# A fused forward-and-backward kernel: two loads re-ordered on one queue, and the last product cut in two

## The chip, the core and the metric

The kernel runs on one core of a Trainium2 chip. Such a core has a matrix engine (TensorE, "PE" in the profile, with its weight loads as "PEld"), a vector engine (VectorE, "DVE"), a scalar engine (ScalarE, "ACT"), GpSimd ("POOL"), and SyncE ("SP"), which here does nothing but issue transfers. Sixteen DMA engines move the data. Operands lie in an on-chip memory of 128 partitions; a matmul writes to PSUM, from which ScalarE or VectorE copies the result. The metric is the device time of one launch in microseconds (us), the lower the better.

## The reference, cut to what matters

Two branches read a layer-normed `x` (2048 rows of 512): a gated convolution along the sequence (branch A) and a bilinear feed-forward layer of width 1376 (branch B). The kernel computes the output and the gradients of nine inputs.

```python
xn = layernorm(A_q)
# branch A
k_shift = sum_t k_pad[:, t:t+S, :] * shift_k[:, ks-1-t]      # ks = 4 taps
kv = k_shift * v
y  = causal_convolution(kv, ssm_k) + kv * ssm_D              # by FFT in the reference
A  = xn * y
# branch B
h  = (xn @ w_gate) * (xn @ w_up)
B  = h @ w_down
out = A_q + A + B
outputs = out, and the gradients to A_q, A_k, A_v, shift_k, ssm_k, ssm_D, w_gate, w_up, w_down
```

In the code below, `out_9` is the gradient to `w_down` (1376 x 512), `out_7` and `out_8` are those to `w_gate` and `w_up` (512 x 1376), `out_5` is that to `ssm_k`, `out_4` that to `shift_k`, `out_0` the output, and `out_1`, `out_2`, `out_3` the gradients to `A_q`, `A_k` and `A_v`.

## The kernel before, in words

The 2048 rows lie as 128 partitions x 16 rows (`R = 16`). In the first 300 us, eight chunks of 256 rows go through the feed-forward layer (`ffn1`, `yb`), and beside them a transform of the convolution's operands runs through DRAM buffers. Two of those buffers matter here: `HDD` holds, for eleven blocks of 128 hidden columns (the last has 96), the hidden values `h` and two gradients; `GD` holds the spectral products.

From 300 us on, `dw()` (L1044) takes the eleven blocks `fb` of `HDD` in turn. For each, `down_grad(fb)` (L1022) makes `pd`, 16 matmuls of 512 columns (`out_9`), and then `pu`, 64 matmuls, gives the gradients of the other two weights (`og`, L1069). Blocks 0 to 5 come by a plain load `load_hb` (L790, into tiles `hb`, two buffers) and are turned on TensorE by `hid_t` (L846, matmuls of L859): parts 0 and 1 of block `fb + 1` behind block `fb`'s `pd`, part 2 in the middle of block `fb + 1`'s own `pd`. Blocks 6 to 10 are turned by the transfer itself (`load_t`, L804, tile `natT`).

Between these, generators on a hand-written cadence (`sides`, L1197) put other work: `inv_y` (L944) turns the spectral products back, by loads `load_g1` (L783, tile `g1`; the profile calls it `g`) and matmuls `pq` (L932): for every four rows `r4` once into `yC`, once into `dd`, which VectorE multiplies by `vb` into `dks` (L962) and by `kb` (L963). `dsk_gram` (L1079) multiplies `dks` by the shifted k (`khC`, matmuls `pk`, L1085), for `out_4`. `ew` (L1180) runs `final(b)` (L1127: `o`, `e`, by VectorE, with the load `bb`) and `bwd(b)` (L1104: `tk`, `dk`), and stores `o`, `e`, `dk` one turn later (`put_late`, L1177).

From 300 us on, transfers are asked for on SyncE's queue, but for two that are on ScalarE's: the last `BX` store, and half of the last `out_9` store (L1039). A scheduler in the framework orders the instructions of each engine by its own estimate of their times; `tc.issue_after(x)` keeps a transfer behind transfer `x`; `tc.high_priority` pulls instructions ahead. Transfers take eight completion semaphores in turn: the ninth waits until the first has landed.

Three places are touched by the change:

- `open_c` (L862) asks, at about 300 us, for `hb` of block 0, for two `g1` tiles, and then for `hb` of block 1.
- `load_kh` (L1156) asks for the shifted k: one load of 2 MB and two small ones. `inv_y` calls it at the end of its turn `r4 = 8` (`R - 8`), and the loads are kept behind the last `g1` load (`LG["g"]`).
- `down_grad(10)`, the last block (96 columns), is the last work of TensorE. Its `pd` is copied out in two halves of 256 columns, one by ScalarE and one by VectorE (L1035 to L1039); the two `og` stores of this block are asked for by SyncE (L1073) just before.

Of the kernel before, what the change touches and what calls it, by code (L numbers as in the profile page):

```python
# [8 lines left out]
BF = mybir.dt.bfloat16  # L9
# [9 lines left out]
D = 512  # L19
F = 1376  # L20
R = 16
P = 128
NC4 = 4
FBLK = [(i * 128, min(128, F - i * 128)) for i in range((F + 127) // 128)]
NFB = len(FBLK)
# [165 lines left out]
def kernel(  # L191
# [24 lines left out]
    nc = tc.nc  # L216
# [14 lines left out]
    def cs(c):  # L231
        return slice(c * 128, (c + 1) * 128)

    def act(o, i):
        nc.scalar.copy(o, i)  # L235
# [10 lines left out]
    HDD = dram.tile([P, NFB, NCH - 1, 3, 256], BF, name="HDD")  # L246
# [5 lines left out]
    def P2(name, shape, dt=F32):  # L252
        return ps2.tile(shape, dt, name=name, tag="p2")

    def P1(name, shape, dt=F32):
        return ps1.tile(shape, dt, name=name, tag="p1")
# [526 lines left out]
    def load_g1(sg, r0):  # L783
        t = CP["b"].tile([P, 2, 4, D], BF, name="g1")
        LG["g"] = nc.sync.dma_start(t[:], GD[sg, :, :, r0:r0 + 4, :])
        return t

    LG = {}

    def load_hb(fb):  # L790
        f0, fw = FBLK[fb]
        t = CP["b"].tile([P, NCH - 1, 3, 256], BF, name="hb")
        nc.sync.dma_start(t[:fw], HDD[:fw, fb])
        hbs[fb] = t

    hbs = {}
# [37 lines left out]
    def nat_h(fb, r):  # L834
        f0, fw = FBLK[fb]
        if fb not in TURNED:
            return nats[fb, 0][:, r, :fw]
        return nats[fb, 0][r // 2][:, 0, r % 2, :] if r < R - 2 else nats[fb, 1][:, 0, r % 2, :fw]

    def nat_d(fb, r):  # L840
        f0, fw = FBLK[fb]
        if fb not in TURNED:
            return nats[fb, 1][:, :, r, :fw]
        return nats[fb, 0][r // 2][:, 1:3, r % 2, :] if r < R - 2 else nats[fb, 1][:, 1:3, r % 2, :fw]

    def hid_t(fb, t):  # L846
        if fb in TURNED:
            return
        f0, fw = FBLK[fb]
        hb = hbs.pop(fb) if t == 2 else hbs[fb]  # L850
        if t == 0:
            nats[fb, 0] = CP["n"].tile([P, R, P], BF, name="nath")
        elif t == 1:
            nats[fb, 1] = CP["n"].tile([P, 2, R, P], BF, name="natd", bufs=2)
        dst = nats[fb, 0] if t == 0 else nats[fb, 1][:, t - 1]
        pt = P2("pt", [P, R, P], BF)
        for r in range(R):
            hs = hb[:fw, r // 2, t] if r < R - 2 else hds[1][:fw, fb, t]
            nc.tensor.transpose(pt[:, r, :fw], hs[:, (r % 2) * 128:(r % 2) * 128 + 128], ident[:fw, :fw])  # L859
        act(dst[:, :, :fw], pt[:, :, :fw])  # L860

    def open_c():  # L862
        for _ in side:
            pass
        gpool["es"].close()
        CP["n"] = ctx.enter_context(tc.tile_pool(name="c1n", bufs=1, reuse_waits="tile"))
        CP["b"] = ctx.enter_context(tc.tile_pool(name="c1b", bufs=2, reuse_waits="tile"))
        load_hb(0)
        pend.extend((load_g1(0, 0), load_g1(1, 0)))
        load_hb(1)  # L870

    def main():
        for ch in range(NCH):
# [22 lines left out]
    for tag in mainit:  # L896
        if tag == "wa":
# [3 lines left out]
            goC = c1.tile([P, R, D], BF, name="goC")  # L901
# [15 lines left out]
    c2b = ctx.enter_context(tc.tile_pool(name="c2b", bufs=2, side="right", reuse_waits="tile"))  # L917
# [10 lines left out]
    def st1p(g, i0, dst):  # L928
        pq = P2("pq", [P, 2, D])
        for i in range(2):  # L930
            for c in range(2):
                nc.tensor.matmul(pq[:, i, :], lhsT=TB.IW[:, c, :], rhs=g[:, c, i0 + i, :], start=(c == 0), stop=(c == 1))  # L932
        act(dst, pq[:])

    def load_vk(r0):
        vb = c2b.tile([P, 2, D], BF, name="vb")
        nc.sync.dma_start(vb[:], v_n[:, r0:r0 + 2, :])
        kb = c2b.tile([P, 2, D], BF, name="kb")
        DKS["kb", r0] = nc.sync.dma_start(kb[:], KS[:, r0:r0 + 2, :])
        return vb, kb  # L940
# [3 lines left out]
    def inv_y():  # L944
        gq = pend
        todo = [(sg, r0) for r0 in range(0, R, 4) for sg in (0, 1)][2:]
        for r4 in range(0, R, 4):
            gy = gq.pop(0)
            vk = [load_vk(r4), load_vk(r4 + 2)]
            for i in range(0, 4, 2):  # L950
                st1p(gy, i, yC[:, r4 + i:r4 + i + 2, :])
            if todo:
                gq.append(load_g1(*todo.pop(0)))
            yield
            gd = gq.pop(0)
            for i in range(0, 4, 2):
                r0 = r4 + i
                vb, kb = vk.pop(0)
                dd = c2b.tile([P, 2, D], BF, name="dd")
                st1p(gd, i, dd[:])  # L960
                with tc.high_priority(offset=SOON):
                    nc.vector.tensor_tensor(dks[:, r0:r0 + 2, :], dd[:], vb[:], op=ALU.mult)  # L962
                    nc.vector.tensor_tensor(kb[:], dd[:], kb[:], op=ALU.mult)  # L963
                DKS[r0] = nc.sync.dma_start(o3_n[:, r0:r0 + 2, :], kb[:])
                if r0 == 2:
                    nc.gpsimd.memset(dks[96:128, R:R + 3, :], 0.0)
                    nc.sync.dma_start(dks[0:112, R:R + 3, :], dks[1:113, 0:3, :])
                    nc.sync.dma_start(dks[112:127, R:R + 3, :], dks[113:128, 0:3, :])
            if todo:
                gq.append(load_g1(*todo.pop(0)))  # L970
            if r4 == R - 8:
                load_kh()
            yield

    def load_gk(rq):
# [45 lines left out]

    def down_grad(fb):  # L1022
        f0, fw = FBLK[fb]
        pd = P1("pd", [P, D])
        for r in range(R):
            nc.tensor.matmul(pd[:fw, :], lhsT=nat_h(fb, r), rhs=goC[:, r, :], start=(r == 0), stop=(r == R - 1))  # L1026
            if r == R // 2 - 1 and fb:
                hid_t(fb, 2)
                if fb + 2 < NFB:
                    load_h(fb + 2)  # L1030
        od = c2b.tile([P, D], BF, name="od")
        if fb + 1 < NFB:
            act(od[:fw], pd[:fw])
            nc.sync.dma_start(out_9[f0:f0 + fw, :], od[:fw])
        else:  # L1035
            for h, cp, q in ((0, act, nc.scalar), (1, dve, nc.sync)):
                hc = slice(256 * h, 256 * h + 256)
                cp(od[:fw, hc], pd[:fw, hc])
                q.dma_start(out_9[f0:f0 + fw, hc], od[:fw, hc])  # L1039

    def load_h(fb):
        (load_t if fb in TURNED else load_hb)(fb)

    def dw():  # L1044
        og = None
        load_hb(2)
        for fb, (f0, fw) in enumerate(FBLK):
            last = fb + 1 == NFB
            if not last:
                down_grad(fb)  # L1050
                yield
                hid_t(fb + 1, 0)
                hid_t(fb + 1, 1)
                yield
                yield
            pu = P2("pu", [P, NC4, 2, P])
            if fb % 2 == 0:
                og = c2b.tile([P, 2, NC4, P], BF, name="og1", tag="dd") if last else c2.tile([P, 2, NC4, 2 * P], BF, name="og")
            q0 = (fb % 2) * P
            for c in range(NC4):  # L1060
                for r in range(R):
                    nc.tensor.matmul(pu[:, c, :, :fw], lhsT=xnC[:, r, cs(c)], rhs=nat_d(fb, r),  # L1062
                                     start=(r == 0), stop=(r == R - 1))
                if c == 1:
                    yield
                    if fb + 1 in TURNED:
                        last_t(fb + 1)
                    yield
            act(og[:, :, :, q0:q0 + fw].rearrange("p t c f -> p c t f"), pu[:, :, :, :fw])  # L1069
            if fb % 2 == 1 or last:  # L1070
                a = f0 - q0
                for t, o in enumerate((out_7, out_8)):
                    LG["og"] = nc.sync.dma_start(o[:, a:f0 + fw].rearrange("(c p) f -> p c f", p=128), og[:, t, :, :q0 + fw])  # L1073
            yield
            if last:
                down_grad(fb)
                yield
# [78 lines left out]
    def load_kh():  # L1156
        khC = c2.tile([P, R + 3, D], BF, name="khC", tag="o5k")
        nc.gpsimd.memset(khC[0:1, 0:3, :], 0.0)
        with tc.issue_after(LG["g"].ins):
            nc.sync.dma_start(khC[:, 3:3 + R, :], k_n)  # L1160
            nc.sync.dma_start(khC[1:113, 0:3, :], k_n[0:112, R - 3:R, :])
            nc.sync.dma_start(khC[113:128, 0:3, :], k_n[112:127, R - 3:R, :])
        KH.append(khC)
# [72 lines left out]
```

## Time and profile before

| what | value |
|---|---|
| device time, median of 3 runs | 479.41 us (476.85 to 480.81) |
| the profiled execution: its own time | 479.29 us |
| its span (first to last instruction) | 477.5 us |
| granted TensorE clock over the span | 0.998 |
| TensorE busy, 300 to 470 us | 168.9 of 170 us |
| moved by DMA, mean | 139.85 MB, 293 GB/s |

A row of the page's part 2 has 40 slices of about 12 us; each digit is a busy share in tenths. A line of the timeline has the start, the time taken (us), the engine (`SPq` and `ACTq` are the queues that issue transfers: that time is the issuing alone), the line of the kernel, the operation, what it writes and reads, its count, and in brackets how long the engine had been idle and what ended that. "To landing" is the time from a transfer's issue until it has arrived.

### The profile page before, as it was taken

What the parts mean: (1) busy time and instruction counts of PE and PEld (TensorE: products, weight loads), DVE (VectorE), ACT (ScalarE), POOL (GpSimd) and SP (SyncE); (2) the same over time, 40 slices, a digit from 0 to 9 for tenths busy, and PEclk for the clock granted to TensorE, in tenths of its full rate; (3) what the DMA queues carried; (4) which work ended last, traced back from release to release, by engine and by line L of the source; (5) the groups of instructions that cost most, each with busy time, mean ns of one, the idle gap of its engine ahead of it and who ended that gap; (6) DMA issues with size and microseconds to landing.
All of it is one profiled execution on the core that took longest, in us unless ns stands there. A gap on an engine that the chain in (4) does not pass through costs nothing.

```text
span 477.5 us, 10282 instructions
## 1 busy us (share of the span) xinstructions
PE 461.4 (97%) x4206; PEld 308.9 (65%) x4247; DVE 339.8 (71%) x610; ACT 304.1 (64%) x356; POOL 13.9 (3%) x30
## 2 busy tenths in 40 slices
PE   7998999999999999999999999999999999999995
PEld 6876765547637538447547753467776787777884
DVE  7889988979447566787857878112147898799892
ACT  4957777749567678879779975275775654333330
POOL 8000000000000000000000000110000000000000
PEclk9999999999999999999999999999999999999999
DMA  9999999998998968968968459998999999999948
GB/s 267 377 373 372 290 286 321 328 313 295 324 292 284 263 189 273 284 193 259 300 218 261 155 198 371 327 366 301 337 371 381 366 304 311 319 284 299 229 166 269
DMA packets 116916, 139.85 MB, mean 293 GB/s; under 512 B 44775, under 2 KB 90248, under 8 KB 115462
## 3 DMA queue, kind: packets, MB, share of 16 engines
q1 hardware_dynamic: 115286, 137.85, 90.8%
q10 hardware_dynamic: 1584, 1.36, 1.0%
q8 instruction: 33, 0.54, 0.5%
q14 instruction: 13, 0.11, 0.1%
HBM read 65.70 MB, written 63.41 MB: 270 GB/s over the span
## 4 chain that ended last, share of the span: by engine, by line
PE 77%; DMA 12%; DVE 6%; issue 1%; SPq 1%; ACT 1%; DVEq 0%; ACTq 0%
PE pu L1062 14%; PE px L555 13%; PE pgu L512 13%; PE pd L1026 8%; PE py L548 6%; PE pdh L518 6%; PE pt L859 3%; PE pq L932 3%; PE ps L584 3%; PE pg L613 3%; DMA ssk<-in_A_ssm_k_dram 3%; PE pf L370 2%; DMA hb<-HDD 2%; DMA x_b<-in_A_q_dram 2%; DMA XN<-x_b 1%
## 5 line engine op out<-in xcount | busy, mean ns | idle before, releaser
L555 PE MATMUL px<-WT,hd 128*128 128x512 bf16 (+1 forms) x340 | 78.6, 379 | 1.6 <-issue 1.4
L1062 PEld LDWEIGHTS <-xnC 128*128 128x128 bf16 x704 | 67.1, 98 | 8.2 <-issue 0.4
L555 PEld LDWEIGHTS <-hd 128*128 128x128 bf16 (+1 forms) x352 | 32.8, 98 | 44.4 <-issue 7.7
L235 ACT CAST gu<-pgu 128x1024 bf16<-128x1024 f32 (+1 forms) x48 | 45.4, 946 | 16.5 <-PE pgu L512 16.2
L235 ACT CAST GO<-pg 128x1024 bf16<-128x1024 f32 x48 | 46.3, 1016 | 13.7 <-issue 7.2
L235 ACT CAST SP<-ps 128x1024 bf16<-128x1024 f32 x47 | 45.6, 1027 | 13.7 <-PE ps L584 11.8
L512 PE MATMUL pgu<-xt,Wu 128*128 128x256 bf16 (+1 forms) x352 | 53.2, 273 | 1.2 <-DVE kn L238 0.6
L600 DVE TENSOR_TENSOR T<-SP 128x2048 bf16<-128x2048 bf16 x24 | 29.4, 1223 | 34.8 <-ACT SP L235 34.7
L512 PE MATMUL pgu<-xt,Wg 128*128 128x256 bf16 (+1 forms) x352 | 52.8, 273 | 0.0
L518 PE MATMUL pdh<-gt,WdT 128*128 128x256 bf16 (+1 forms) x352 | 46.9, 273 | 0.1
L235 ACT CAST fst<-pf 128x1024 bf16<-128x1024 f32 x44 | 42.8, 1032 | 5.8 <-issue 2.3
L1062 PE MATMUL pu<-natd,xnC 128*128 128x256 bf16 x384 | 43.9, 273 | 0.0
L512 PEld LDWEIGHTS <-Wu 128*128 128x128 bf16 (+1 forms) x352 | 33.0, 100 | 15.5 <-issue 10.6
L548 PE MATMUL py<-Wd,hd 128*128 128x512 bf16 (+1 forms) x167 | 40.2, 380 | 0.8 <-issue 0.5
L518 PEld LDWEIGHTS <-WdT 128*128 128x128 bf16 (+1 forms) x352 | 34.9, 100 | 4.8 <-issue 0.2
L512 PEld LDWEIGHTS <-Wg 128*128 128x128 bf16 (+1 forms) x352 | 34.8, 100 | 3.8 <-DMA Wg<-in_B_w_gate_dram 0.2
L1062 PE MATMUL pu<-natT,xnC 128*128 128x256 bf16 (+1 forms) x280 | 32.3, 267 | 0.0
L533 DVE TENSOR_TENSOR hd<-gu,dh 128x1024 bf16<-128x1024 bf16 (+1 forms) x48 | 30.8, 642 | 0.8
L532 DVE TENSOR_TENSOR hd<-gu 128x512 bf16<-128x512 bf16 (+1 forms) x48 | 19.1, 398 | 16.1 <-ACT gu L235 16.1
L548 PEld LDWEIGHTS <-hd 128*128 128x128 bf16 (+1 forms) x176 | 16.5, 98 | 20.8 <-issue 3.1
L235 ACT CAST og<-pu 128x1024 bf16<-128x1024 f32 (+1 forms) x11 | 10.9, 993 | 29.7 <-PE pu L1062 22.1
L600 DVE TENSOR_TENSOR U<-SP 128x2048 bf16<-128x2048 bf16 x24 | 29.2, 1219 | 0.0
(175 smaller groups left out, 680.9 us busy)
## 6 DMA issues: line engine op xcount, KB each, us to landing
HDD<-hd SPq DMA_DIRECT2D x35, 384.0 KB, 4.4
FD<-fst SPq DMA_DIRECT2D x24, 512.0 KB, 5.2
X<-FD SPq DMA_DIRECT2D x24, 512.0 KB, 5.2
GD<-GO SPq DMA_DIRECT2D x24, 512.0 KB, 3.7
g<-GD SPq DMA_DIRECT2D x11, 1024.0 KB, 8.0
hb<-HDD SPq DMA_DIRECT2D x6, 1344.0 KB, 11.2
bb<-BX SPq DMA_DIRECT2D x8, 512.0 KB, 5.6
BX<-bx SPq DMA_DIRECT2D x7, 512.0 KB, 3.9
```

The lines of the kernel that those rows point to most:

```text
L235: nc.scalar.copy(o, i)
L512: nc.tensor.matmul(pgu[:w, i, t, :], lhsT=W[:, c, f0:f0 + w], rhs=xt[:, :, c, :], start=(c == 0), stop=(c == NC4 - 1))
L518: nc.tensor.matmul(pdh[:w, i, :], lhsT=WdT[:, c, f0:f0 + w], rhs=gt[:, :, c, :], start=(c == 0), stop=(c == NC4 - 1))
L532: nc.vector.tensor_tensor(hd[:fw, fb0:fb0 + n, 0, :], gu[:fw, :n, 0, :], gu[:fw, :n, 1, :], op=ALU.mult)
L533: nc.vector.tensor_tensor(hd[:fw, fb0:fb0 + n, 1:3, :], gu[:fw, :n], dh[:fw, :n].unsqueeze(2).to_broadcast((fw, n, 2, 256)), op=ALU.mult)
L548: nc.tensor.matmul(py[:], lhsT=hd[:fw, fb, 0, ss], rhs=Wd[:fw, fb, :], start=(fb == 0), stop=(fb == NFB - 1))
L555: nc.tensor.matmul(px[:], lhsT=hd[:fw, fb, t, ss], rhs=W[:fw, fb, :], start=(t == 1 and fb == 0), stop=(t == 2 and fb == NFB - 1))
L584: nc.tensor.matmul(ps[32 * q:32 * q + 32, a, :], lhsT=TB.EF[64 * a:64 * a + 64, 4 * g + q, ri].rearrange("p k j -> p (k j)"), rhs=X[64 * a ...
L600: tt(W[:].rearrange("p c a d -> p c (a d)"), A[:, i:i + 1].rearrange("p c a d -> p c (a d)").to_broadcast((P, 2, 2 * D)), B[:].rearrange(" ...
L613: nc.tensor.matmul(pg[q // 2][64 * a:64 * a + 64, q % 2, :], lhsT=TB.EI[32 * q:32 * q + 32, 2 * g + a, yi].rearrange("p k c -> p (k c)"), ...
L1026: nc.tensor.matmul(pd[:fw, :], lhsT=nat_h(fb, r), rhs=goC[:, r, :], start=(r == 0), stop=(r == R - 1))
L1062: nc.tensor.matmul(pu[:, c, :, :fw], lhsT=xnC[:, r, cs(c)], rhs=nat_d(fb, r), start=(r == 0), stop=(r == R - 1))
```

## The change

```diff
 def load_hb(fb):
-        nc.sync.dma_start(t[:fw], HDD[:fw, fb])
+        LG[fb] = nc.sync.dma_start(t[:fw], HDD[:fw, fb])
...
 def open_c():
         load_hb(0)
+        load_hb(1)
         pend.extend((load_g1(0, 0), load_g1(1, 0)))
-        load_hb(1)
...
 def inv_y():
         for r4 in range(0, R, 4):
             gy = gq.pop(0)
+            if r4 == R - 4:
+                load_kh()
             vk = [load_vk(r4), load_vk(r4 + 2)]
...
-            if r4 == R - 8:
-                load_kh()
             yield
...
 def down_grad(fb):
+        if fb + 1 == NFB:
+            for h, q in ((0, nc.sync), (1, nc.scalar)):
+                hc = slice(256 * h, 256 * h + 256)
+                pd = P1("pd", [P, 256])
+                for r in range(R):
+                    nc.tensor.matmul(pd[:fw, :], lhsT=nat_h(fb, r), rhs=goC[:, r, hc], start=(r == 0), stop=(r == R - 1))
+                od = c2b.tile([P, D], BF, name="od")
+                act(od[:fw, :256], pd[:fw])
+                q.dma_start(out_9[f0:f0 + fw, hc], od[:fw, :256])
+            return
...
-        if fb + 1 < NFB:
-            act(od[:fw], pd[:fw])
-            nc.sync.dma_start(out_9[f0:f0 + fw, :], od[:fw])
-        else:
-            for h, cp, q in ((0, act, nc.scalar), (1, dve, nc.sync)):
-                hc = slice(256 * h, 256 * h + 256)
-                cp(od[:fw, hc], pd[:fw, hc])
-                q.dma_start(out_9[f0:f0 + fw, hc], od[:fw, hc])
+        act(od[:fw], pd[:fw])
+        nc.sync.dma_start(out_9[f0:f0 + fw, :], od[:fw])
...
 def dw():
-                    LG["og"] = nc.sync.dma_start(o[:, a:f0 + fw]...)
+                    LG["og"] = (nc.scalar if last else nc.sync).dma_start(o[:, a:f0 + fw]...)
...
 def load_kh():
-        with tc.issue_after(LG["g"].ins):
+        with tc.issue_after(LG[5].ins):
```

- The load of block 1's `hb` goes ahead of the two `g1` loads.
- The three loads of the shifted k are asked for one turn of `inv_y` later (`r4 = 12`), and are kept behind block 5's `hb` load. In the changed program SyncE's order there is: last `g1` load, `o` and `e` stores, `bb` load, block 5's `hb`, `out_9`'s store, then the three `khC` loads, then `vb` and `kb`.
- The last block's `pd` is two products of 16 matmuls of 256 columns in place of one of 16 of 512. Both halves are copied by ScalarE; SyncE stores the first and ScalarE the second. The last block's two `og` stores move from SyncE's queue to ScalarE's, ahead of these copies.
- As the scheduler works from its own estimates, VectorE's order changes too, in one place: the two first instructions of `final(2)` (`o`, `e`) and its addition of `bb` move up among the end of `final(1)` and `bwd(0)`, and the `dks` and `kb` products of `r4 = 12`, which stood before `bwd(1)`, come right after it. TensorE's order differs in the last product alone, ScalarE's in the last copies and stores.

More of the change, by code (lines that the diff above doesn't have):

```diff
@@ L1072, in dw @@
                 for t, o in enumerate((out_7, out_8)):
-                    LG["og"] = nc.sync.dma_start(o[:, a:f0 + fw].rearrange("(c p) f -> p c f", p=128), og[:, t, :, :q0 + fw])
+                    LG["og"] = (nc.scalar if last else nc.sync).dma_start(o[:, a:f0 + fw].rearrange("(c p) f -> p c f", p=128), og[:, t, :, :q0 + fw])
             yield
```

## The prediction, made before the changed kernel was run

> **What bounds the kernel now.** First the page: busy time by engine, and the DMA row.
>
> ```profile
> PE 461.4 (97%) x4206; PEld 308.9 (65%) x4247; DVE 339.8 (71%) x610; ACT 304.1 (64%) x356; POOL 13.9 (3%) x30
> DMA  9999999998998968968968459998999999999948
> ```
>
> TensorE is busy for 97% and the DMA engines nearly as long. All edits lie after 300 us, so I asked for TensorE's waits from 320 us to the end. The answer is one line:
>
> ```profile
> PE pd L1026 <- issue: 0.2, 1, 0.2
> ```
>
> So no load makes TensorE wait there; before that, at 308.36 us, 0.21 us was spent on block 0's `hb`, which the change does not touch. What remains of the two moved loads is margins. The timeline gives when TensorE first reads each of them:
>
> ```profile
> 318.40 1.89 PE L932 MATMUL pq<-g,IW 128*128 128x512 bf16 x8
> 320.12 0.94 PE L859 MATMUL pt<-ident,hb 128*128 128x128 bf16 x14
> ...
> 384.69 0.94 PE L859 MATMUL pt<-ident,hb 128*128 128x128 bf16 x14
> ...
> 390.06 1.94 PE L1085 MATMUL pk<-khC,dks 128*64 128x256 bf16 x32
> ```
>
> These are the first `g`, block 1's `hb`, block 5's `hb`, and the first use of `khC`.
>
> **Block 1's `hb` ahead of `g`: 0.** By issue time plus time to landing, the queue delivers in order: `hb` 0 at 308.3 (300.15 + 8.2), `g` at 310.8 and 313.4, `hb` 1 at 316.6 (302.39 + 14.2). The same bytes in the new order: `hb` 1 lands 3.2 us after `hb` 0, at 311.5, the first `g` 2.5 later, at 314.0, the second at 316.6. They are needed at 320.1, 318.4 and 325.4 us: margins of 8.6, 4.4 and 8.8 us where they were 3.5, 7.6 and 12. Nothing waited and nothing will. The next load in that queue, block 2's `hb`, needs a buffer that TensorE frees at 315, and stays there.
>
> **`khC` behind block 5's `hb`: 0 on TensorE.** SyncE's queue there:
>
> ```profile
> 363.66 0.53 SPq L785 DMA_DIRECT2D g<-GD  x1
> 364.24 0.60 SPq L1160 DMA_DIRECT2D khC<-in_A_k_dram  x1
> ...
> 366.08 0.38 SPq L1177 DMA_DIRECT2D out_dram<-o  x1
> ...
> 367.77 0.49 SPq L793 DMA_DIRECT2D hb<-HDD  x1
> ...
> 375.91 0.33 SPq L937 DMA_DIRECT2D vb<-in_A_v_dram  x1
> ```
>
> The transfers are full there (DMA share 0.92 to 1.06 from 365 to 385), so landings follow the order of bytes. Before: `g` 369.6, `khC` 375.9 and 376.6, `hb` 5 at 383.4 (367.77 + 15.6), which leaves 1.3 us before 384.69; `vb`, `kb`, `vb` at 384.4, 385.0 and 385.7. After: `o`, `e` and `bb` go ahead of 2.4 MB of `khC`, 0.65 us for each 256 KB (`vb` to `kb`) or 1.1 (`khC` to `o`, which VectorE waited for until 377.7), so `o` lands at 370.3 to 370.7, `e` by 371.8, `bb` by 374. `hb` 5 can be asked for when TensorE frees its buffer (366.6) and lands near 376.5, 8 us early. `khC` is asked for behind `out_9`'s store, which stood at 369.7, and lands at about 383.7, 6.4 us before 390.06. `vb` and `kb` end where they did, as the sum of bytes is the same. The 5.9 us that SyncE waited before `vb` for `khC`'s landing (it takes the completion semaphore of the transfer eight before it) goes too, but the data could not have come sooner. In a slower execution 1.3 us of margin on `hb` 5 could be too little and 6.4 on `khC` would not be; here I count nothing.
>
> **VectorE's new order: 0, with a thin margin.** Before:
>
> ```profile
> 371.62 0.69 DVE L1151 TENSOR_TENSOR e<-e,goC 128x1024 bf16<-128x1024 bf16 x1
> ...
> 377.72 0.69 DVE L1135 TENSOR_TENSOR o<-xnC,yC 128x1024 bf16<-128x1024 bf16 x1 [0.84 <-DMA out_dram<-o]
> 378.95 0.69 DVE L1139 TENSOR_TENSOR e<-goC,yC 128x1024 bf16<-128x1024 bf16 x1 [0.53 <-DMA out_dram<-e]
> 380.22 0.69 DVE L1136 TENSOR_TENSOR o<-o,bb 128x1024 bf16<-128x1024 bf16 x1 [0.58 <-DMA bb<-BX]
> ...
> 387.65 0.69 DVE L962 TENSOR_TENSOR dks<-dd,vb 128x1024 bf16<-128x1024 bf16 x1
> ```
>
> The three waits (1.95 us) were for transfers queued behind `khC`, and go. But the `dks` products of `r4 = 12` now come after `bwd(1)`. From 371.62 I add the distances between starts: `o`, `e`, `e` and `o`+`bb` 0.61 each; two `bwd` of 4.6; the rest of `final(2)` 5.6. That puts the last `dks` product at 390.0, done at 390.7, where it was done at 388.3. The gram takes 32 matmuls in 1.87 us, row by row, and reads rows 14 and 15 in its last eighth, from 391.7. The margin falls from 3.4 to 1.0 us. GpSimd's order is unchanged. On SyncE's queue the second `kb` store (390.81) waits for its product until 391.4 now, and `dk`, `bb` and `og` behind it may come 0.5 us late; VectorE alone waits for these. Then `o` of `final(3)` waits for a store asked for behind the turning load at 389.2, and the next `bb` (396.97) comes when it did or 0.5 later, so VectorE's gain of 1.95 us is gone by 397.
>
> **The tail: -0.3.**
>
> ```profile
> 471.87 2.07 SPq L1073 DMA_DIRECT2D out_dram<-og  x2
> 472.38 0.37 ACT L235 CAST od<-pd 96x256 bf16<-96x256 f32 x1 [2.60 <-PE pd L1026]
> 472.78 0.36 ACTq L1039 DMA_DIRECT2D out_dram<-od  x1
> 472.78 0.42 DVE L238 CAST od<-pd 96x256 bf16<-96x256 f32 x1 [4.42 <-ACT od L235]
> 474.04 0.64 SPq L1039 DMA_DIRECT2D out_dram<-od  x1
> ```
>
> TensorE ends at 472.3. VectorE's copy waits for ScalarE's, then SyncE is still issuing `og`, and the last store leaves 1.26 us after ScalarE's. In the semaphores' records `og` lands at 476.0 and 476.4, ScalarE's half at 475.8, SyncE's at 476.6; the closing waits take the other 0.9 us to 477.5. After: ScalarE copies `og` until 469.8 and issues its two stores by 470.6 (0.4 each, as on ScalarE's queue at 472.78) or 471.8 (1.0 each, as on SyncE's at 471.87). The first half of `pd` ends at 470.6, its copy at 472.2 at the latest, and SyncE stores it once `dk` is issued (471.8). The second half ends at 472.4: 32 matmuls of 256 columns cost what 16 of 512 do, since `pu`'s 32 took 3.49 us and `pd`'s 16 took 3.47. Its copy (0.37) and issue follow at 472.8, as before. So the issuing is 1.26 us shorter. Does the end follow? The DMA engines' rows say hardly:
>
> ```profile
> 472.00:473.00 1.00, 0.34 (x2) 0.00 (x0) 0.22 (x1) 0.37 (x1) 0.00 (x0) 1.00 1.01 397
> ...
> 475.00:476.00 1.00, 0.00 (x0) 0.00 (x0) 0.00 (x0) 0.00 (x0) 0.00 (x0) 0.58 1.01 178
> ```
>
> The share is 0.97 to 1.09 in every microsecond from 470 to 476: the engines work off one backlog (`o5t`, `dk`, `og`) without a gap, and the bytes stay. By that row the gain is 0. The other bound is a last half that lands 3.0 us after its issue, as ScalarE's did (472.78 to 475.8), which gives 475.9 instead of 476.6: -0.75. I take -0.3, nearer the full engines.
>
> A rule of the Trainium skill says otherwise of the halves: "TensorE: Matmul & The Clock Gate", section "The mechanism", has weight loads run beside matmuls only when their row groups differ. By it sixteen more weight loads would be paid in full; `pu`'s 3.49 us with its 32 loads of 98 ns beside it disagree.
>
> The sum, on the profiled execution: 479.29 + 0 + 0 + 0 - 0.3 = **479.0 us**, 0.4 under the median of 479.41.
>
> **Rivals.**
>
> *The tail gives all of its issue time:* the small `og` packets go between `o5t`'s large ones and cost nothing. For it: DMA share above 1 at 470 to 472, so packets overlap somewhat. Against: in 475 to 476 two queues were active and the rate was 178 GB/s. It is -0.75, 478.5 us. Chance 0.15.
>
> *Hidden stalls of other executions go:* the three runs spread from 476.85 to 480.81, and block 5's `hb` had 1.3 us to spare. Were half of the upper spread such stalls, the median falls to some 478. Chance 0.12. Nothing in this trace shows one.
>
> *Slower, VectorE's order:* `o` now stands ahead of `e`+`goC`, `bwd(0)` and, further on, the `dks` products, so a late store of `final(0)` holds them all, and TensorE waits at the first gram. It decides from a landing at 372.6 (371.62 + 1.0), 8.4 us after the issue at 364.2; beyond, each microsecond costs one. At the landing before (377.7) it would be 5.1 us: 484.4 us. Against: 256 KB right behind a `g` that lands at 369.6. Chance 0.06 for over 0.5 us, half of that for over 4.
>
> *Slower, paid weight loads:* 16 x 0.098 = 1.6 us on TensorE, so the last store is issued at 474.4, lands at 477.4 and ends 0.8 later than now: 480.1 us. Chance 0.04.
>
> *Nothing changes that can be measured, since no wait was there to remove:* that is my forecast, with 0.63.
>
> **How the numbers follow.** The three runs spread over 0.8%, so 1%, 4.8 us, is about what a measurement can tell from no change. All cases but the far end of the order's stay within it: slower 0.04 (0.03 from that end, 0.01 for two small ones together), faster 0.05 (the outer part of the hidden stalls' 0.12, where they are longer than the three runs show), same 0.91. The range takes the tail's bounds (-0.75 to +0.8) and the spread of the runs about their median (-2.6 to +1.4): 476.0 to 481.4.
>
> **What would show it.** Right: TensorE without a wait from 320 us on; `hb` 5 landing near 376 and `khC` near 384; VectorE without the three waits at 377 to 381; the last landing between 475.9 and 476.6. Wrong: a wait of `pk` on `dks` or `khC` near 390, a gap before `pq` at 318, `pd`'s 32 matmuls over 3.6 us, or DMA share under 0.9 before the end.

## The result, and the profile after

| kernel | device time, median | lowest to highest | runs |
|---|---|---|---|
| before | 479.47 us | 476.85 to 482.54 | 22 |
| after | 481.70 us | 479.03 to 484.63 | 22 |

The ratio after to before is 1.0042, 95% interval 1.0024 to 1.0059: the change makes the kernel slower by 2.0 us. The forecast was 479.0 and its range ended at 481.4; the median lies 0.3 above that, and the movement has the other sign. It is within the 1% that was called "same".

The profiled execution of the changed kernel took 479.56 us (span 477.7), the second fastest of the 22. That it is as short as the profile of before is luck of its first part: TensorE comes to the matmuls `pq` of `r4 = 12` 1.57 us earlier in it. First the line of before, then that of the changed kernel:

```profile
375.12 1.89 PE L932 MATMUL pq<-g,IW 128*128 128x512 bf16 x7
...
373.55 1.89 PE L932 MATMUL pq<-g,IW 128*128 128x512 bf16 x8
```

From TensorE's `pq` at 318.40 (316.82 in the changed kernel) to this one the two take the same time, 56.7 us. From this `pq` to the end of the span are 102.4 us before and 104.2 after. So two profiles are better compared by times counted from this `pq`; where the text does so, it says it. The page's busy times and the DMA row of the changed kernel:

```profile
PE 465.4 (97%) x4263; PEld 310.9 (65%) x4263; DVE 339.0 (71%) x609; ACT 304.3 (64%) x357; POOL 13.9 (3%) x30
...
DMA  8999999988998968967977459998999999999959
```

As before: TensorE is at 97%. Of TensorE's waits from 320 us on there is again one line:

```profile
PE pu L1066 <- ACT natd L235: 0.2, 1, 0.2
```

No load makes TensorE wait, as forecast. The timeline of VectorE, of the changed kernel, answers to the lines of before with the three waits and the last `dks` product:

```profile
369.72 0.69 DVE L1139 TENSOR_TENSOR o<-xnC,yC 128x1024 bf16<-128x1024 bf16 x1
...
373.27 0.69 DVE L1140 TENSOR_TENSOR o<-o,bb 128x1024 bf16<-128x1024 bf16 x1
...
388.10 0.68 DVE L964 TENSOR_TENSOR dks<-dd,vb 128x1024 bf16<-128x1024 bf16 x1
...
392.40 0.69 DVE L1139 TENSOR_TENSOR o<-xnC,yC 128x1024 bf16<-128x1024 bf16 x1 [3.00 <-DMA out_dram<-o]
...
397.17 0.69 DVE L1140 TENSOR_TENSOR o<-o,bb 128x1024 bf16<-128x1024 bf16 x1 [2.25 <-DMA bb<-BX]
```

The waits near 377 to 381 are gone, the addition of `bb` comes 6.9 us earlier (373.3, was 380.2; 5.4 counted from `pq`), and by 397 all of it is given back: VectorE waits 3.00 us for a store of `o` and 2.25 for `bb`, and adds the next `bb` at 397.17, where it was 396.99. By the clock of the span that is what the prediction said; counted from `pq` this addition is 1.8 us late. The same kernel's timeline for SyncE's queue shows what both wait for:

```profile
364.90 0.34 SPq L793 DMA_DIRECT2D hb<-HDD  x1
...
367.78 0.43 SPq L1164 DMA_DIRECT2D khC<-in_A_k_dram  x1
...
374.27 0.33 SPq L939 DMA_DIRECT2D kb<-KS  x1
381.47 6.88 SPq L817 DMA_TRANSPOSE natT<-HDD  x1
388.44 0.52 SPq L1181 DMA_DIRECT2D out_dram<-o  x1
...
391.56 0.52 SPq L1128 DMA_DIRECT2D bb<-BX  x1
392.17 1.33 SPq L1077 DMA_DIRECT2D out_dram<-og  x2
```

SyncE is held for 6.88 us in issuing block 6's turning load (6.08 in the profile of before). Everything behind it (`o`, `e`, `kb`, `dk`, `bb`, `og`) waits for that. By the clock of the span the landings in the semaphores' records are near the forecast: `o` at 369.7 (370.3 to 370.7 were expected), `e` at 369.9, `bb` at 371.0, `khC` at 383.1 and 383.3 (383.7), `vb`, `kb`, `vb` at 383.7, 384.4 and 385.0; block 5's `hb` left no record. Counted from `pq`, `vb`, `kb` and `vb` land 0.9 us later than before (384.4, 385.0 and 385.7).

At the end of the timeline:

```profile
468.51 1.42 ACTq L1077 DMA_DIRECT2D out_dram<-og  x2
...
471.12 0.37 ACT L235 CAST od<-pd 96x256 bf16<-96x256 f32 x1 [0.78 <-PE pd L1029]
471.52 0.35 ACTq L1032 DMA_DIRECT2D out_dram<-od  x1
472.70 1.19 SPq L1032 DMA_DIRECT2D out_dram<-od  x1
```

and in the rows of the DMA engines for the same stretch (the last three columns are the granted clock, DMA share and GB/s):

```profile
472.00:473.00 1.00, 0.00 (x0) 0.00 (x0) 0.00 (x0) 0.00 (x0) 0.00 (x0) 1.00 1.07 313
...
475.00:476.00 1.00, 0.00 (x0) 0.00 (x0) 0.00 (x0) 0.00 (x0) 0.00 (x0) 0.94 1.02 338
```

ScalarE's stores leave early, the last store is SyncE's at 472.70 (was 474.04), and the engines still work off one backlog without a gap until 476.

So TensorE has no wait that counts in this execution, as the prediction had it. But counted from `pq`, TensorE's last matmul is 0.3 us later than in the profile of before, VectorE's last product 2.8 and the end 1.8. The runs of one kernel differ by more than that (those of before by 5.7 us), so where the 2.0 us come from had to be found by experiments.

### The profile page after: what moved, and what is told of

It is laid out like the page before. It is cut to its first block, busy times and chain, and to the rows that moved or that the text cites. A ratio compares the mean times of both kernels' runs of the same rounds, so it can differ in the third digit from the quotient of the medians.

```text
span 477.7 us, 10351 instructions
## 1 busy us (share of the span) xinstructions
PE 465.4 (97%) x4263; PEld 310.9 (65%) x4263; DVE 339.0 (71%) x609; ACT 304.3 (64%) x357; POOL 13.9 (3%) x30
## 4 chain that ended last, share of the span: by engine, by line
PE 75%; DMA 11%; DVE 10%; ACT 1%; issue 1%; SPq 1%; DVEq 0%; ACTq 0%
PE px L555 15%; PE pu L1066 13%; PE pgu L512 13%; PE py L548 7%; PE pdh L518 6%; PE pd L1036 5%; PE ps L584 3%; PE pg L613 3%; DMA ssk<-in_A_ssm_k_dram 3%; PE pf L370 3%; PE pq L932 2%; PE pt L859 2%; DMA x_b<-in_A_q_dram 2%; PE po L1001 2%; DMA out_dram<-o 1%; DMA out_dram<-og 1%
## 5 line engine op out<-in xcount | busy, mean ns | idle before, releaser
L555 PE MATMUL px<-WT,hd 128*128 128x512 bf16 (+1 forms) x352 | 81.0, 380 | 0.0
L548 PE MATMUL py<-Wd,hd 128*128 128x512 bf16 (+1 forms) x176 | 41.4, 380 | 0.0
L600 DVE TENSOR_TENSOR U<-SP 128x2048 bf16<-128x2048 bf16 x24 | 29.2, 1218 | 0.0
```

Of the source, the lines that this page charges most:

```text
L548: nc.tensor.matmul(py[:], lhsT=hd[:fw, fb, 0, ss], rhs=Wd[:fw, fb, :], start=(fb == 0), stop=(fb == NFB - 1))
L555: nc.tensor.matmul(px[:], lhsT=hd[:fw, fb, t, ss], rhs=W[:fw, fb, :], start=(t == 1 and fb == 0), stop=(t == 2 and fb == NFB - 1))
L600: tt(W[:].rearrange("p c a d -> p c (a d)"), A[:, i:i + 1].rearrange("p c a d -> p c (a d)").to_broadcast((P, 2, 2 * D)), B[:].rearrange(" ...
```

## The experiments

Each kernel was timed 6 to 12 times beside 11 to 35 runs of the kernel before on the same chip. The letters of the theories belong to each group; where a letter comes back it is explained again. The three parts of the change are called *hb* (`open_c`), *kh* (the place of `khC`'s loads) and *tail* (`down_grad`, `og`).

### Which part costs

*e1_hb*, the first part alone:

```diff
         load_hb(0)
+        load_hb(1)
         pend.extend((load_g1(0, 0), load_g1(1, 0)))
-        load_hb(1)
```

> Only block 1's hb load goes ahead of the two g loads; all else as before. The whole change measured +2.0 us (ratio 1.0042). Theory V (the moved khC load leaves VectorE's late chain behind, and that chain's stores end the kernel): no change here, ratio 1.000 within 0.002. Theory T (the tail's stores on ScalarE's queue cost it): also 1.000. Theory H (the first g now lands too late or the loads at 300 us collide): 1.002 to 1.004, with a wait of TensorE before pq near 318 us.

Measured: 480.33 us against 480.45, ratio 0.9990 (0.9963 to 1.0018). No cost.

*e2_kh*, the second part alone:

```diff
+            if r4 == R - 4:
+                load_kh()
             vk = [load_vk(r4), load_vk(r4 + 2)]
...
-            if r4 == R - 8:
-                load_kh()
...
-        with tc.issue_after(LG["g"].ins):
+        with tc.issue_after(LG[5].ins):
```

> Only the khC loads are moved behind block 5's hb; VectorE's order changes with it. Theory V: the whole loss, 1.003 to 1.005, with VectorE's last instruction 1 us or more later against the start of SyncE's last stores than before. Theory T or H: 1.000 within 0.002.

Measured: 481.90 us, ratio 1.0032 (1.0013 to 1.0050).

*e3_tail*, the third part alone (the halves of `pd`, and):

```diff
-                    LG["og"] = nc.sync.dma_start(o[:, a:f0 + fw]...)
+                    LG["og"] = (nc.scalar if last else nc.sync).dma_start(o[:, a:f0 + fw]...)
```

> Only the last block: product in halves, both copied by ScalarE, its og stores on ScalarE's queue. Theory T: 1.003 to 1.005. Theory V: 0.998 to 1.000 (the time from SyncE's last-but-one dk store to the end was 13.8 us before and 12.8 in the changed kernel, so the tail by itself should gain up to 1 us, 0.2%).

Measured: 479.94 us, ratio 0.9991 (0.9966 to 1.0015).

*e4_hbkh*, the edits of e1 and e2 together:

> Both load moves, without the tail. Theory V: as the khC move alone or up to 0.002 above the whole change, 1.004 to 1.006. Theory T: 1.000. Theory H: as the hb move alone.

Measured: 481.20 us, ratio 1.0035 (1.0008 to 1.0063). The move of `khC` carries all of the cost that can be told from none, some 1.5 us; *hb* and *tail* are no change that can be measured.

### What the move of khC does

The timeline of e2 (its profiled execution took 482.98 us) has what the one of the full change lacks:

```profile
372.93 0.69 DVE L1135 TENSOR_TENSOR o<-xnC,yC 128x1024 bf16<-128x1024 bf16 x1 [0.39 <-DMA out_dram<-o]
...
381.84 9.31 SPq L817 DMA_TRANSPOSE natT<-HDD  x1
...
390.85 0.41 PE L1085 MATMUL pk<-khC,dks 128*64 128x256 bf16 x4 [0.49 <-DVE dks L964]
392.05 0.41 PE L1085 MATMUL pk<-khC,dks 128*64 128x256 bf16 x4 [0.80 <-DVE dks L964]
...
395.40 1.33 SPq L1073 DMA_DIRECT2D out_dram<-og  x2
...
401.94 1.01 ACT L235 CAST og<-pu 128x1024 bf16<-128x1024 f32 x1 [3.61 <-DMA out_dram<-og]
403.01 1.94 PE L1085 MATMUL pk<-khC,dks 128*64 128x256 bf16 x32 [0.63 <-ACT og L235]
```

Two things. The gram's `pk` waits for the late `dks` products (1.29 us): the margin that the prediction had put at 1.0 us. They are late because VectorE's `o` at 372.93 had to wait for a store of `o` that landed at 372.90, right behind the last `g`; from there VectorE runs without a wait to the last of these products. And the turning load holds SyncE for 9.31 us, the `og` stores of blocks 2 and 3 go out at 395.4, ScalarE's next `og` copy, which needs their buffer, waits 3.61 us for them to land, and TensorE waits 0.63 us behind ScalarE. Against that, in the timeline of the kernel before:

```profile
383.05 6.08 SPq L817 DMA_TRANSPOSE natT<-HDD  x1
...
393.10 1.11 SPq L1073 DMA_DIRECT2D out_dram<-og  x2
...
399.24 1.01 ACT L235 CAST og<-pu 128x1024 bf16<-128x1024 f32 x1 [1.37 <-DMA out_dram<-og]
```

The wait is there too, 1.37 us, and TensorE does not feel it. Which of the two it is, was the next question: the products' order on VectorE, or SyncE's queue.

*f1_order*: the move of `khC`, with VectorE's `bwd(1)` held behind the `kb` product of `r4 = 12` (`pr`, kept in `DKS["v"]`).

```diff
+            with tc.issue_after(DKS["v"].ins):
+                nc.vector.tensor_tensor(t[:], src, w, op=ALU.mult)
```

> khC moved as in the change, but VectorE's dks and kb products of r4 = 12 stand ahead of bwd(1) again, as they did before. Two theories for the 1.5 us that the khC move alone costs. Theory O (order): the products come about 2 us later, the gram's pk waits for dks and the kb stores go out late; then this kernel is back at the time before, ratio 0.998 to 1.001, and no wait of pk on dks is left. Theory Q (queue): khC's 2.4 MB now stand close ahead of the turning load on SyncE's queue, which holds SyncE until they have landed; then the order is of no account and the ratio stays at 1.002 to 1.005.

Measured: 481.23 us, ratio 1.0021 (0.9995 to 1.0047). The waits of `pk` on `dks` are gone; one of 0.72 us behind `og` is left. It decides neither way.

*f2_nat_late* and *f3_kh_nat_late*: block 6's turning load behind the next `bb`, without and with the move of `khC`.

```diff
-        first = {NFB - 5: lambda: DKS["kb", R - 2], ...
+        first = {NFB - 5: lambda: LG["bb"], ...
```

> The kernel before with one thing changed: block 6's turning load is issued behind the next bb load instead of right behind the kb loads, so that the stores of o, e, kb and dk and that bb go out before it. The turned tile is first read at 414, so it has time. Theory Q: bb lands some 3 us earlier (near 394 instead of 397), VectorE's two waits of final(3) shrink, and VectorE and with it the end come 1 to 3 us sooner: ratio 0.994 to 0.998. Theory O: nothing of the products' order is touched, ratio 0.999 to 1.001.

> khC moved as in the change, and block 6's turning load behind the next bb as in the run beside it. Theory Q: the move of khC costs nothing once no store waits behind the turning load, so this is as fast as the kernel with the turning load alone moved, within 0.1%, and faster than the kernel before. Theory O: it stays 0.3% above that one.

Measured: 484.23 us, ratio 1.0081 (1.0049 to 1.0112), and 487.25 us, 1.0142 (1.0103 to 1.0181). Theory Q expected a gain and fell. `bb` did land earlier (addition at 394.7), but now the `og` stores stood right behind the turning load. In f3's timeline:

```profile
398.53 1.08 SPq L1073 DMA_DIRECT2D out_dram<-og  x2
...
403.69 1.01 ACT L235 CAST og<-pu 128x1024 bf16<-128x1024 f32 x1 [7.01 <-DMA out_dram<-og]
404.75 3.44 PE L1085 MATMUL pk<-khC,dks 128*64 128x256 bf16 x32 [4.02 <-ACT og L235]
```

This miss showed one path of the cost. In the thirteen profiles in which TensorE waits here, its wait is ScalarE's wait less 2.98 or 2.99 us: 3.61 and 0.63 in e2, 5.24 and 2.26 in f2, 7.01 and 4.02 in f3. TensorE has 3 us to spare behind the `og` copy, of which the profile of before used 1.37. (In f4, next, TensorE is late itself: ScalarE waits 4.93 us and TensorE not at all.)

*f4_kh_early*: `khC` one turn earlier than before.

```diff
-            if r4 == R - 8:
+            if r4 == 4:
                 load_kh()
```

> The kernel before with khC asked for in the second round of inv_y instead of the third, some 15 us earlier, ahead of block 4's hb. The scheduler moves more with it: VectorE's products stand ahead of most of final(2), and a store of o goes ahead of the turning load. Theory Q: o, e and bb no longer queue behind khC and nothing more stands ahead of the turning load, so 0 to 1 us is gained: ratio 0.998 to 1.000. Theory O: the products are earlier than before, so no loss, ratio about 1.000. A ratio over 1.002 speaks for a load of khC costing wherever full queues are.

Measured: 485.60 us, ratio 1.0102 (1.0064 to 1.0141). TensorE waits 4.2 us for a `g`: earlier, the 2.4 MB stand ahead of loads with no margin. It moves too much else to tell the theories apart.

*g1_nat7* and *g2_kh_nat7*: block 7's turning load behind the next `bb`, without and with the move of `khC`; *g4_all_nat7*: the same line in the kernel with the whole change.

```diff
-        first = {NFB - 5: lambda: DKS["kb", R - 2], NFB - 3: ...
+        first = {NFB - 5: lambda: DKS["kb", R - 2], NFB - 4: lambda: LG["bb"], NFB - 3: ...
```

> Delaying block 6's turning load made the kernel slower by 0.8%, so theory Q (that the stores and bb right behind it carry the cost) has fallen. In the ten profiles so far the fifth bb addition of VectorE starts 7.4 to 7.8 us after the SECOND turning load (block 7's) lets go of SyncE, which is 2.7 us after the last g ahead of it has landed, and the span ends 62 to 64 us after that addition. Theory R (release): this release sets the end, not TensorE. Here, in the kernel before, block 7's turning load alone is put behind the next bb load, so that three stores and that bb no longer wait for its release. Theory R: the fifth addition comes 4 to 7 us earlier (408 to 412 instead of 415.6), and the end comes earlier until TensorE's end (472 + 5) bounds it: ratio 0.992 to 0.998. If TensorE bounds the kernel as predicted, nothing changes: 0.999 to 1.001. If what is pushed behind the turning load matters more, as with block 6's: over 1.003.

> khC moved as in the change, and block 7's turning load behind the next bb as in the run beside it. Theory R: khC's move delays the release of SyncE by the two turning loads; with VectorE's bb no longer behind the second release, at most half of the 1.5 us is left against the run beside it (0 to 0.8 us). Theory O (VectorE's order) or a cost ahead of the first turning load: 1 to 2 us above the run beside it.

> The whole change, and block 7's turning load behind the next bb. Theory R: as the same kernel without the other two edits or 0.3 us better, since with VectorE early the tail's shorter issue counts: ratio 0.992 to 0.999. If TensorE bounds the kernel: 1.002 to 1.005, as the change.

Measured: g1 480.57 us, ratio 0.9998 (0.9972 to 1.0024); g2 482.21 us, 1.0028 (1.0002 to 1.0053); g4 481.09 us, 1.0001 (0.9976 to 1.0027). Theory R fell as a theory of one chain. In g1's timeline VectorE's fifth addition of `bb` comes 4.2 us earlier than the 415.55 of before (2.8 counted from `pq`), as expected, and another `og` copy then holds TensorE:

```profile
411.36 0.68 DVE L1136 TENSOR_TENSOR o<-o,bb 128x1024 bf16<-128x1024 bf16 x1
...
457.65 2.69 PE L1062 MATMUL pu<-natT,xnC 128*128 128x256 bf16 x14 [2.59 <-ACT og L235]
```

That wait is not the work of this edit alone, since e1's timeline, with block 7's load in its old place, has it too:

```profile
456.69 1.69 PE L1062 MATMUL pu<-natT,xnC 128*128 128x256 bf16 x14 [2.70 <-ACT og L235]
```

And VectorE's lead does not last: its eighth addition of `bb` is at 454.59 in g1 and at 449.87 in before. g2 is 0.3% above g1, as e2 is above the kernel before; the intervals overlap, so this only speaks for a cost ahead of the second turning load. g4's interval reaches from below the kernel before to g2, so nothing is read from it.

*g3_kh_mid*: `khC` behind `o`, `e` and `bb`, but ahead of block 5's `hb`; VectorE, ScalarE and TensorE in the order of e2.

```diff
-            if r4 == R - 8:
-                load_kh()
...
             f()
+            if len(FL) == 1 and 2 in FL and not KH:
+                load_kh()
...
-        with tc.issue_after(LG["g"].ins):
+        with tc.issue_after(LG["bb"].ins):
```

> khC is asked for behind o, e and bb but ahead of block 5's hb. Every instruction of VectorE, ScalarE and TensorE stands in the same order as with the change's place of khC; only SyncE's queue differs, by khC against hb and the store of od. Theory O: VectorE's order carries the cost, so this is as slow as the khC move alone: ratio 1.002 to 1.005. Theory B (bytes): khC's landing beside the vb and kb loads and the start of the turning load carries it; here khC lands near 378 again and hb near 383, so the ratio is 0.997 to 1.001.

Measured: 482.06 us, ratio 1.0028 (1.0005 to 1.0052). By the time alone theory B falls (it is not that `khC` lands beside `vb` and `kb`). But g3's timeline has a stall that none of the kernels so far has, as block 5's `hb`, again behind `khC`, comes too late:

```profile
386.59 0.95 PE L859 MATMUL pt<-ident,hb 128*128 128x128 bf16 x14 [1.41 <-DMA hb<-HDD]
```

These 1.41 us are as much as g3's loss (0.28%, 1.3 us). They come from one execution, the slowest of g3's twelve, so whether B is refuted stays open. What is common to all kernels with the cost is that `o`, `e` and `bb` stand ahead of `khC`, and VectorE's order.

*h1_order_alone* and *h2_queue_alone* part these two; *h3_kh_again* repeats e2 beside them. h1 lowers the priority of the two products of `r4 = 12` and leaves SyncE's queue as it was; h2 has the new queue, with VectorE held in the old order by f1's edit and by keeping the first two products of `final(2)` behind `bwd(0)`, whose last product is `DKS["w"]`. The first two lines of the diff are h1's, the others h2's.

```diff
-                with tc.high_priority(offset=SOON):
+                with tc.high_priority(offset=SOON if r4 < R - 4 else -500):
...
+        with tc.issue_after(DKS["w"].ins) if b == 2 else ExitStack():
+            tt(o[:], xnC[:, rb], yC[:, rb], op=ALU.mult)
```

> The kernel before, SyncE's queue unchanged to the last instruction, khC in its old place; only the priority of the dks and kb products of r4 = 12 is lowered, and with that VectorE's instructions stand in the order that the change gives them. Theory O (order): ratio 1.002 to 1.005, as the khC move. Theory S (SyncE's queue, o, e and bb ahead of khC): 0.999 to 1.001.

> khC moved as in the change, SyncE's queue as the change has it; VectorE's instructions are held in the order of before (final(2) behind bwd(0), the products of r4 = 12 ahead of bwd(1)). Theory O: 0.998 to 1.001. Theory S: 1.002 to 1.005.

> The khC move alone once more, as the anchor for the two runs beside it: 1.002 to 1.005 under both theories.

Measured: h1 480.13 us, ratio 1.0018 (0.9995 to 1.0041); h2 480.78 us, 1.0005 (0.9983 to 1.0027); h3 480.60 us, 1.0024 (1.0003 to 1.0045). Neither part alone shows a cost that can be told from none, both together do. The times do not split it. The traces do so in part:

| profile | SyncE free, us after `kb` landed | `og` copy waits | TensorE waits for it | `pk` waits for `dks` |
|---|---|---|---|---|
| queue of before: before | 27.6 | 1.37 | 0 | 0 |
| e1_hb | 27.5 | 2.01 | 0 | 0 |
| e3_tail | 27.7 | 3.27 | 0.28 | 0 |
| g1_nat7 | 27.8 | 3.52 | 0.54 | 0 |
| h1_order_alone | 27.8 | 3.51 | 0.52 | 0 |
| h4_hb_tail (below) | 28.4 | 2.31 | 0 | 0 |
| queue of the change: after | 28.6 | 2.79 | 0 | 0 |
| e2_kh | 28.1 | 3.61 | 0.63 | 1.29 |
| e4_hbkh | 29.4 | 5.87 | 2.88 | 1.11 |
| f1_order | 29.1 | 3.70 | 0.72 | 0 |
| g2_kh_nat7 | 28.3 | 3.44 | 0.46 | 0 |
| g3_kh_mid | 29.2 | 3.48 | 0.49 | 0 |
| g4_all_nat7 | 28.7 | 4.02 | 1.04 | 0 |
| h2_queue_alone | 28.2 | 3.67 | 0.69 | 0 |
| h3_kh_again | 29.2 | 5.44 | 2.46 | 0.23 |

The first column is the time from the landing of the second `kb` of `r4 = 8` (359 to 363 us, ahead of all that the move touches) to the end of the issue of block 6's turning load. The means are 27.8 us over six profiles and 28.8 over nine: the new queue frees SyncE 1.0 us later. TensorE's wait behind `og` has means of 0.22 and 1.04 us, its wait for `dks` 0 and 0.29. That is 1.1 us together; the ratios of the nine kernels have a mean of 1.0024, 1.15 us. That the two agree is no proof. The table has the `og` copy near 400 us alone: for the later one TensorE waits 2.70 us in e1, 2.59 in g1 and 2.30 in g4. With these and the 1.41 us for `hb` in g3, the means are 1.1 us over the six profiles and 1.7 over the nine, so the difference shrinks to 0.6. These are single executions with a wide scatter; the two paths are shown, and what they cost is not. The wait for `dks` is seen only where both parts are present, in three of seven such profiles, and in none of f1, h1 and h2.

Both paths start at one place. The last `g` load, the last transfer ahead of all that the move re-orders, lands 6.9 us after its issue in the mean of the six profiles (6.0 to 7.7) and 8.0 in that of the nine (6.4 to 8.8). In the nine, the store of `o` lands 0.4 to 1.2 us behind it, and in six of the seven with both parts (all but after) VectorE waits for that store, 0.39 to 1.31 us.

Nor need a wait of TensorE be time at the end. In eleven of the fifteen profiles the span ends 8.1 to 8.2 us behind VectorE's last product; in before, g1, e4 and g4 it is 9.0 to 9.3, with TensorE 4.0 to 5.2 us from the end. Counted from `pq`, VectorE's fourth addition of `bb` starts after 23.3 us in the mean of the six (21.9 to 24.3) and after 25.0 in that of the nine (23.6 to 26.9). So VectorE's own chain may carry the cost as well, as theory V of e1 and e2 had it; no run parts it from TensorE's waits.

### Can another queue carry the stores?

*h4_hb_tail*: the two parts without cost, `khC` where it was.

> Block 1's hb ahead of g and the last down gradient in halves, khC in its old place. Both theories: 0.997 to 1.001, since each of the two showed 0.999 alone.

Measured: 479.60 us, ratio 0.9990 (0.9974 to 1.0006). It cannot be told from the kernel before.

*i1_og_gpsimd*, the `og` stores alone, and *i2_stores_gpsimd*, the `og`, `o`, `e` and `dk` stores with the edits of h4 (here Theory H is that the held queue carries the cost). The last two lines of the diff are i2's alone; there the last pair of `og` stays on ScalarE's queue:

```diff
-                    LG["og"] = nc.sync.dma_start(...)
+                    LG["og"] = (nc.sync if last else nc.gpsimd).dma_start(...)
...
-            LG["late"] = nc.sync.dma_start(dst, t[:])
+            LG["late"] = nc.gpsimd.dma_start(dst, t[:])
```

> The kernel before, with the og stores (but the last pair) issued by GpSimd, which is 3% busy, instead of SyncE, so that no turning load holds them. Theory H (held queue): ScalarE's og copy no longer waits 2 to 5 us for out_dram<-og, TensorE's waits at pk and pu behind it go, and the end, which VectorE's chain then sets, comes 0 to 2 us sooner: ratio 0.996 to 1.000, more if bb and the o stores come sooner as well. If GpSimd's descriptors are slow to come, the og buffer is free later and the ratio is over 1.002.

> Block 1's hb ahead of g and the last down gradient in halves, khC in its old place, and the stores of og (but the last pair), o, e and dk all issued by GpSimd. SyncE keeps the loads, the kb, od and o5t stores. Theory H: VectorE no longer waits for o's and e's buffers behind a turning load and bb is asked for earlier, so VectorE and TensorE both end earlier: ratio 0.990 to 0.998. If the DMA engines' backlog alone sets the end, whichever queue carries it: 0.998 to 1.002. If GpSimd's issuing is slow (27 more DMAs), over 1.002.

Measured: i1 488.06 us, ratio 1.0165 (1.0137 to 1.0193); i2 514.04 us, 1.0666 (1.0617 to 1.0715). The first half of the expectation held: in i1 the `og` copy at 399 of before runs at 393.6 without waiting for a store, one later copy waits (4.4 us), and TensorE waits for no `og`. The end did not follow. In i1's timeline TensorE's last matmuls end earlier than in the profile of before (471.74 against 472.34), VectorE's last product 6.9 us later, and the span ends at 485.0:

```profile
471.15 0.59 PE L1026 MATMUL pd<-goC,nat 128*96 128x512 bf16 x2
...
474.56 0.69 DVE L1116 TENSOR_TENSOR dk<-dk,tk 128x1024 bf16<-128x1024 bf16 x1
```

VectorE waits 17.6 us for `bb` in i1 (11.2 in before) and 7.7 for the stores of `o` (3.7). In i2 it waits 39.9 us for the stores of `o` and `e`, and TensorE 15.4 us for one `dks`. What makes these transfers late when GpSimd issues was not tried.

## Why the prediction failed

**What bounds the kernel: this is where it went wrong first.** From TensorE's 97% and its one wait of 0.2 us, the prediction took TensorE for the bound in every execution. In e1's timeline the last lines of VectorE's products and TensorE's matmuls are

```profile
472.08 0.69 DVE L1116 TENSOR_TENSOR dk<-dk,tk 128x1024 bf16<-128x1024 bf16 x1
...
473.13 0.59 PE L1026 MATMUL pd<-goC,nat 128*96 128x512 bf16 x2
```

and the span ends at 480.9: 8.1 us behind VectorE and 7.2 behind TensorE. It is 8.1 behind VectorE in after, e1, e2, f1 and h3 as well, with TensorE 6.6 to 7.3 us ahead of the end; in before, e4 and g1 it is 5.2, 4.5 and 4.5 behind TensorE and 9.0 to 9.2 behind VectorE. Two chains end close together, both hang on SyncE's queue, and the profile of before is an execution in which neither was late: its 102.4 us from `pq` to the end are the least of the fifteen (the others have 104.1 to 107.8). That its time, 479.29 us, lay near the median hid this, since it was late at `pq`.

**Block 1's hb ahead of g, 0: right.** 0.9990, and no wait near 318 in any profile.

**khC on TensorE's own loads, 0: right.** No `pk` waits for `khC` anywhere. "`vb` and `kb` end where they did, as the sum of bytes is the same" is the sentence that failed: measured from the landing of the `kb` before them, SyncE is free of the turning load 1.0 us later in the nine profiles with the new queue, and in after itself `vb` and `kb` land 0.9 us late, counted from `pq`. What is late first is `g`, whose landing at 369.6 the prediction took as given: 8.0 us after its issue in the mean of the nine, 6.9 in that of the six. Why is open. In the fourth to eighth microsecond after the landing of `kb`, while `g` comes in, the engines move 303 GB/s in the mean against 393, but in the next eight 430 against 351, so the bytes missing there are made up before the turning load ends.

**VectorE's new order, 0 with a thin margin: the failed term.** Two of its sentences fell. The margin of 1.0 us for the `dks` products was overrun in three executions, and in two of them TensorE waited for over 1 us; it was priced at 0 since the one trace at hand kept it. What overran it is the rival with that name, a late store of `o`, which was to decide from a landing at 372.6 on and to cost a microsecond for each one beyond. Put on the clock of before by their `pq`, the landings of `o` are 374.1 in e2, 373.9 in e4 and 372.9 in h3, and TensorE waits 1.29, 1.11 and 0.23 us for `dks`; in after, g2 and g4 they are 371.3, 372.6 and 372.0, and it does not wait. (In g3, at 373.5, TensorE had itself lost 1.41 us to `hb`.) So that rival was right in its path and its price. Its chance, 0.06 for over 0.5 us, was too small (two of seven profiles), as the argument against it, 256 KB "right behind a `g` that lands at 369.6", leaned on the quickest `g` of the fifteen profiles (5.96 us). And of the stores and loads behind the `kb` stores it says that "VectorE alone waits for these". ScalarE waits for `og`, and TensorE for ScalarE, once `og` is over 2.98 us late. In place of the 0, TensorE waits 1.1 us more in the mean at these two places; how much of that reaches the end is not shown. "VectorE's gain of 1.95 us is gone by 397" is right to 0.2 us by the clock of the span, but counted from `pq` the `bb` at 397 comes 1.8 us late in after, where at most 0.5 was allowed, and the means of the nine and the six profiles are 1.7 apart.

**The tail, -0.3: not contradicted.** 0.9991 is -0.4 us with an interval of 1.2 us to each side, and h4 agrees. The bound that went by the full DMA engines held: the share is 1.01 to 1.07 until 476. SyncE's half of `pd` left last, 0.9 us later than the 471.8 worked out, since SyncE was at `dk` until 472.6. The 32 matmuls of `pd` took 3.65 us from the first start to the last end, where the 16 took 3.61 by the same reading (468.73 to 472.34). The mark of 3.6 was passed, by the reading and not by the halves: sixteen weight loads at the prediction's 98 ns paid in full would have made 5.2, and at the 123 ns that this product's loads take in the profile 5.6. So the rule that the prediction quoted from the Trainium skill ("TensorE: Matmul & The Clock Gate", "The mechanism") does not hold for these loads.

**Hidden stalls of other executions.** The prediction gave them 0.12 as a gain, on block 5's `hb`. Stalls that the profile of before does not show exist, but at another place: behind `og`, where the move of `khC` makes the one near 400 us longer. For block 5's `hb` TensorE waits only in g3 (1.41 us) and i2 (5.07).

## What to carry to other kernels

A wait that costs nothing in the one profile is a margin: find the engine behind it, subtract, and ask of every reordering what it takes of that margin. Here ScalarE's 1.37 us for `og` stood in the trace of the kernel before, and 3 us was the point at which TensorE began to pay. When a transfer holds the queue that issues it, the list of what stands behind must be followed to the last engine for each entry, as the next one in line may be the one without slack. A landing read from one profile is one draw: the last `g` took 6.0 to 8.8 us from issue to landing, and a margin of 1.0 us behind it needs that range, not one value. And two profiles are best compared from a point that the change has not reached yet, here TensorE's `pq` at 375, and not from the start of the span: that start hid 1.6 us.

## What the runs showed of the hardware

- A turning load holds SyncE until the loads ahead of it are in. Its issue ended 3.3 to 3.4 us behind the landing of the last recorded `vb` ahead of it in before, after and e1 to e4 (389.1 and 385.7 in before, 391.1 and 387.8 in e2), so that the issue took 6.1 to 9.8 us for block 6 and 7.8 to 11.6 for block 7.
- Moving stores from SyncE to GpSimd, which was 3% busy, cost 1.7% for ten `og` stores (i1), and 6.7% with the 24 of `o`, `e` and `dk` as well (i2), though it took them out of the held queue.
